# Linear attention and a multiplicative FFN: seven-product gates for two more chunks, sums kept in PSUM, one-instruction minima, and a new order

## The chip, the cores and the metric

The kernel runs on one core of one Trainium2 chip. The core has five engines that follow their own instruction queues: TensorE (PE, with its weight loads shown apart as PEld), VectorE (DVE), ScalarE (ACT), GpSimd (POOL) and SyncE (SP), of which POOL here only starts transfers and SP starts transfers alone. The metric is the time of one execution on the device in microseconds; the lower the better. A change is judged by the median of several runs against the kernel before.

## The reference

Eight sequences of 576 tokens go through a linear attention of 8 heads of 64, and the 4608 rows that come out go through a feed-forward block whose two halves are multiplied:

```python
def phi(x):
    return np.where(x > 0, x, np.exp(x) - 1.0) + 1.0
q_p, k_p = (phi(q), phi(k))
kv = np.einsum('bhsd,bhse->bhde', k_p, v)
z = np.sum(k_p, axis=2)
num = np.einsum('bhsd,bhde->bhse', q_p, kv)
den = np.einsum('bhsd,bhd->bhs', q_p, z)[..., None] + 1e-06
attn = num / den            # (8, 8, 576, 64), then rows of 512
a = x @ w1                  # (4608, 512) @ (512, 1024)
b = x @ w2
h = a * b @ w3              # 1024 x 1024
out = h @ w_out             # 1024 -> 512
```

## The kernel before

The rows are handled in nine chunks of 512. Chunk b below 8 holds the first 512 rows of sequence b; the last 64 rows of all eight sequences form chunk 8. Inputs and outputs are float32, the products are bf16 with float32 sums in PSUM. `w3 @ w_out` is made once, at the start, and kept as `wf_sb`, so a chunk needs two gate products with w1 and w2 and one output product.

The program is not scheduled by a tool: a long string, ORDER, lists its steps, and each engine gets its instructions in the order in which the steps stand there. A step is a letter, the chunk, and a part. A "+" behind a step moves its elementwise work to another engine (its transfers to POOL's queue). The letters that matter here:

- L, M, N and R load k, q, v and the 64-row tails of a sequence; each big load is 512 KB into one of 13 buffers of the pool `ld`. T and D are transposing copies from SBUF to SBUF, started by SP, S and H store rows of the output. SP works through its transfers in the order of the string.
- x, y, z (for k) and X, Y, Z (for q) make phi as min(exp(x), max(x, 0) + 1): ACT's exponential (line 179), DVE's maximum (line 184), DVE's minimum (line 209, two instructions of 128x512 for each half of the heads). v casts the values to bf16 (line 215, ACT).
- K sums k and v over the sequence on PE into `kvp` and ACT copies it to SBUF. A is a normalisation of 128 rows: PE writes numerator and denominator into the PSUM tile `nd`, DVE adds 1e-6 (line 324), takes the reciprocal (325) and multiplies (326).
- F is one gate unit of 128 of the 1024 hidden columns for 512 rows: 4 + 4 matmuls of 128x512 (line 362), an ACT copy of a to SBUF (367), a DVE product with b (368). Chunks 0 to 5 are done with eight F each (for two of chunk 0's and chunk 1's sixteen units the same work is split into steps h and i).
- G is the other way to make gates, used for chunks 6, 7 and 8: the matrices are cut into 2 x 2 blocks and seven block products, with sums and differences of blocks, take the place of eight. For each of four column blocks q there are products 1 to 7, each with four matmuls of 128x256 (line 422), for a and b side by side in one PSUM bank. Products 1, 3, 5 and 7 pile up in one bank (`gu`); after 1 and 3 ACT copies the state to SBUF (line 450). Products 4 and 6 pile up in another bank, product 2 had a bank of its own (`gt`). Sums of an SBUF copy and a bank are DVE's (line 454), and m steps multiply a by b from SBUF (465). Product 7's a half is copied by ACT (458) and multiplied by DVE with its b half in PSUM (459). The block differences come from steps e (weights, line 396) and d (rows, 407).
- O is an output unit of 128 rows: eight matmuls of 128x512 (line 536) and a copy.

PSUM has eight banks: four for F and for G's `gt` banks, two for G's `gu` and O's sums, and a pair for `nd` and `kvp`. The SBUF sums of G live in a ring of 12 half buffers cut from six `ld` buffers.

Of the kernel before, what the change touches and what calls it, by code (L numbers as in the profile page):

```python
# [8 lines left out]
F32 = mybir.dt.float32  # L9
# [11 lines left out]
def kernel(  # L21
# [41 lines left out]
    ones = consts.tile([P, 2], BF16)  # L63
    w1_sb = wpool.tile([P, KC, DFF], BF16)
# [134 lines left out]
    def phi_min(name, b, g):  # L199
# [7 lines left out]
        e, y = (t.rearrange("p (c u j d) -> p c u j d", c=2, u=2, d=D) for t in (e, y))  # L207
        for c in range(2):
            nc.vector.tensor_tensor(out=p[0][:, 2 * g + c].rearrange("p j u d -> p u j d"),  # L209
                                    in0=e[:, c], in1=y[:, c], op=ALU.min)  # L210
# [60 lines left out]
    def q_tr(b, g, alt):  # L271
# [9 lines left out]
        for i in range(2):  # L281
# [4 lines left out]
            out=qts[b, 0][:, 2 * g:2 * g + 2, :].rearrange("p i (j t) -> p (i j) t", t=P), in_=tp)  # L286

    def nat(b, j):
# [35 lines left out]
        nc.vector.tensor_scalar_add(out=r[rows], in0=v4[:, :, :, D], scalar1=1e-6)  # L324
# [110 lines left out]
    def g_unit(c, q, i):  # L435
# [3 lines left out]
        a, m, name, first = ((), ((0, 0, 0), (0, 0, 0), "u", True), ((0, 0, 1), (0, 1, 0), "t", True),  # L439
# [8 lines left out]
        if i in (1, 3, 4):  # L448
            s = st["s", i] = fsm("gs")
            nc.scalar.copy(out=s, in_=t)  # L450
        elif i in (2, 5, 6):
            s = st["c", i] = fsm("gc")
            o = st["s", {2: 1, 5: 4, 6: 3}[i]]
            nc.vector.tensor_tensor(out=s, in0=o, in1=t, op=ALU.add)  # L454
            ring.append(o)
        else:
            s = fsm("ga")
            nc.scalar.copy(out=s[:, 0], in_=t[:, 0])
            nc.vector.tensor_mul(out=abs_[c][:, q + 4, 0:HN], in0=s[:, 0], in1=t[:, 1])
            ring.append(s)  # L460

    def g_mul(c, q, i, alt):
        s = cs_[c, q]["c", i]
        f, r = {2: (q, 0), 5: (q + 4, 1), 6: (q, 1)}[i]
# [121 lines left out]
    A1.4 x2.1 F1.7 F1.6 x2.2 y2.2 z2.2 N2.1 y3.2 x3.2 O0.3 F1.0 Y2.0 X2.0 Z2.0 N2.0 y2.1 F1.1 v2.1+  # L586
    R2.1+ z2.1 L2.0 y2.0 v2.2 F1.5 R3.1+ x2.0 z2.0 M3.0 v2.0 F1.4 O0.2 X3.0 K2 Y3.1 v3.2+ Z3.1 O0.1
    Y3.0 Z3.0 T2.0 A2.3 F1.2 A2.2 N3.0 F1.3 v3.0 L3.1 z3.2 L3.0 x3.0 x3.1 y3.0 S0.1 y3.1 O0.0 N3.1
    T3.0 A2.1 R6.0+ v3.1 O1.1 z3.0 A2.0 O1.0 D2.0 R4.0+ S1.0 z3.1 K3 O1.2 A3.0 O1.3 A3.3 F2.5 F2.3
    A3.2 F2.0 M5.1 Y5.1 R5.1+ R4.1+ y4.2 S1.1 F2.2 M4.1 A3.1 R5.0+ D3.0 x4.2 z4.2 M4.0 F2.1 Y4.1  # L590
    N4.1 F2.4 R6.1+ L4.1 e0.0 A2.4 v4.2 L4.0 F2.6 e0.2 F2.7 X5.1 Z5.1 A3.4 F3.3 X4.0 Y4.0 Z4.0 O2.3+
    X4.1 y5.2 v4.1 y4.1 F3.1 y6.2 Z4.1 x4.1 F3.4 z4.1 v5.2 y4.0 x4.0 F3.0 N4.0 z4.0 F3.5 v4.0 O2.2+
    M5.0 X5.0 K4 v6.2+ e0.1 T4.0 F3.7 x5.2 z5.2 L5.1 x5.1 Y5.0 Z5.0 y5.1 F3.2 S0.0 A4.1 F3.6 L5.0
    y5.0 O2.1 N5.0 x5.0 A4.0 v5.0 O2.0 z5.1 N5.1 S2.1 A4.2 T5.0 v5.1 O3.3 z5.0 A4.3 D4.0 O3.2+ K5
    S3.1 O3.1 A5.3 M6.1 O3.0 A5.0 F4.0 X6.1 A5.2 F4.7 M6.0 X6.0 Y6.0 Z6.0 D3.1 F4.2 F4.4 A5.1 F4.5
    e1.0 F4.3 L6.1 y6.1 x6.1 A4.4 R7.0 L6.0 y6.0 y7.2 D5.0 F4.1 x6.0 F4.6 z6.0 Y6.1 Z6.1 F5.6 x6.2
    z6.2 z6.1 F5.5 N6.1 v6.1 N6.0 A5.4 e1.1 e1.3 M7.0 X7.0 F5.7 S2.0 F5.4 Y7.0 O4.2+ v6.0 K6 O4.3
# [132 lines left out]
```

## Time and profile before

| what | value |
|---|---|
| time, median of 3 runs | 246.97 us (246.8 to 249.23) |
| the profiled execution | 247.36 us |
| its span, first to last instruction | 245.6 us |
| mean granted TensorE clock | 0.993 |
| HBM read and written | 38.80 MB and 9.44 MB |

The profile is one execution. A stretch of time is given from the start of the span. A row of the instruction groups has the line, engine, operation, tiles and shape, the count, then busy time in us, the mean of one in ns, and behind the bar the engine's idle time ahead of these instructions with what ended it. A row of the waits has who waited, for whom, the sum in us, how often, and the longest. Neighbours on one engine overlap a little at their ends, so a group's busy time may be below its count times its mean.

### The profile page before, as it was taken

The page shows a single profiled execution, that of the slowest core. Times are in us where ns is not written, and L with a number is a line of the kernel's source. Part 1 is how long each engine was busy: PE and PEld are TensorE (multiplying, and loading weights), DVE is VectorE, ACT ScalarE, POOL GpSimd, SP SyncE. Part 2 cuts the span into 40 slices and gives each one's busy share as a digit, 9 for nine tenths or more (in the row PEclk, how much of TensorE's full clock was granted, in tenths as well). Part 3 has the DMA queues.
Part 4 walks back from the last instruction along what each step waited for, and adds up shares of the span by engine and source line. Part 5 has one row for each costly group of instructions (what it writes and reads, how often), then busy time and mean ns, then how long its engine had stood idle before and what let it go on. Part 6 is the DMA issues. An engine that isn't in the chain of part 4 may idle for free.

```text
span 245.6 us, 4278 instructions
## 1 busy us (share of the span) xinstructions
PE 229.7 (94%) x1548; PEld 133.2 (54%) x1548; DVE 184.7 (75%) x425; ACT 136.4 (56%) x222; POOL 44.8 (18%) x73
## 2 busy tenths in 40 slices
PE   0689968999999999999999999999999999999994
PEld 0345555654454554444545444454498686788542
DVE  3227979677698837989794589958999996989721
ACT  2207777658775715498663456736776285455220
POOL 8445467660000096200000000000000000000000
PEclk9999997999999999999999999999999999999999
DMA  6999999999869799798997989989980151040074
GB/s 152 192 201 299 297 250 243 198 274 280 274 126 350 152 247 313 166 348 225 275 308 153 256 221 242 280 231 328 209 247 0 23 144 29 0 175 0 3 171 171
DMA packets 65461, 49.43 MB, mean 201 GB/s; under 512 B 34016, under 2 KB 60384, under 8 KB 65440
## 3 DMA queue, kind: packets, MB, share of 16 engines
q1 hardware_dynamic: 54560, 36.71, 55.4%
q0 software_dynamic: 10736, 12.33, 25.1%
q8 instruction: 12, 0.20, 0.3%
q10 hardware_dynamic: 144, 0.13, 0.2%
q14 instruction: 9, 0.07, 0.1%
HBM read 38.80 MB, written 9.44 MB: 196 GB/s over the span
## 4 chain that ended last, share of the span: by engine, by line
PE 83%; DMA 13%; ACT 2%; issue 1%; POOL 0%; ACTq 0%; POOLq 0%
PE o_ps L536 25%; PE a_ps L362 17%; PE b_ps L362 17%; PE gu L422 9%; PE gt L422 6%; DMA q<-in_q_dram 5%; DMA k<-in_k_dram 5%; PE nd L310 4%; DMA wt_sb<-in_moe_w_out_dram 3%; PE kvp L245 2%; ACT e L179 1%; PE o_ps L561 1%; PE kvp L249 1%; PE xtp L341 1%; POOL w3b L137 0%
## 5 line engine op out<-in xcount | busy, mean ns | idle before, releaser
L536 PE MATMUL o_ps<-wf_sb,ab 128*128 128x512 bf16 x280 | 64.7, 379 | 0.0
L362 PEld LDWEIGHTS <-w_sb 128*128 128x128 bf16 x384 | 36.6, 98 | 40.2 <-issue 0.6
L362 PE MATMUL a_ps<-xt,w_sb 128*128 128x512 bf16 x192 | 50.8, 382 | 0.0
L362 PE MATMUL b_ps<-xt,w_sb 128*128 128x512 bf16 x192 | 50.2, 379 | 0.0
L536 PEld LDWEIGHTS <-ab 128*128 128x128 bf16 x280 | 26.9, 98 | 29.1 <-DVE ab L465 0.3
L368 DVE TENSOR_TENSOR ab<-a_sb,b_ps 128x512 bf16<-128x512 f32 x48 | 32.4, 684 | 13.0 <-PE b_ps L362 6.5
L367 ACT COPY a_sb<-a_ps 128x512 f32<-128x512 f32 x48 | 27.5, 585 | 21.5 <-PE a_ps L362 20.2
L538 ACT COPY o_sb<-o_ps 128x512 f32<-128x512 f32 x27 | 15.6, 586 | 34.6 <-PE o_ps L536 24.9
L326 DVE TENSOR_TENSOR xn<-nd,r 128x512 bf16<-128x512 f32 x30 | 20.7, 691 | 1.0
L422 PEld LDWEIGHTS <-spare 128*128 128x128 bf16 x192 | 18.6, 97 | 2.4
L179 ACT ACTIVATE e<-q 128x1024 bf16<-128x1024 f32 x16 | 16.8, 1058 | 5.0 <-DMA q<-in_q_dram 4.9
L310 PE MATMUL nd<-kv,qt 128*128 128x130 bf16 (+1 forms) x160 | 15.9, 221 | 2.8 <-DVE xn L326 1.7
L454 DVE TENSOR_TENSOR spare<-spare,gt 128x512 f32<-128x512 f32 x24 | 16.0, 682 | 2.8 <-ACT spare L450 2.3
L310 PEld LDWEIGHTS <-qt 128*128 128x128 bf16 (+1 forms) x160 | 11.5, 99 | 11.6 <-DVE xn L326 3.0
L154 PE MATMUL wf_ps<-wt_sb,w3t 128*128 128x512 bf16 x64 | 16.1, 394 | 1.1 <-DMA wt_sb<-in_moe_w_out_dram 0.8
L179 ACT ACTIVATE e<-k 128x1024 bf16<-128x1024 f32 x16 | 16.9, 1060 | 0.2 <-DMA k<-in_k_dram 0.2
L450 ACT COPY spare<-gu 128x512 f32<-128x512 f32 x24 | 13.4, 590 | 3.4 <-PE gu L422 2.8
L422 PEld LDWEIGHTS <-w_sb 128*128 128x128 bf16 x144 | 14.0, 98 | 2.4
L465 DVE TENSOR_TENSOR ab<-spare 128x256 bf16<-128x256 f32 x36 | 13.7, 419 | 0.1
L114 POOL DMA_DIRECT2D qk32r<-in_q_dram x12 | 7.6, 636 | 33.5 <-ACT o_sb L538 30.9
L324 DVE TENSOR_SCALAR r<-nd 128x8 f32<-128x8 f32 (+1 forms) x38 | 6.1, 162 | 10.0 <-PE nd L310 9.9
L209 DVE TENSOR_TENSOR qj<-e,y 128x512 bf16<-128x512 bf16 x32 | 12.1, 421 | 1.7 <-ACT e L179 0.9
(87 smaller groups left out, 301.9 us busy)
## 6 DMA issues: line engine op xcount, KB each, us to landing
out_dram<-o_sb SPq DMA_DIRECT2D x15, 512.0 KB, 4.3
q<-in_q_dram SPq DMA_DIRECT2D x13, 512.0 KB, 6.8
k<-in_k_dram SPq DMA_DIRECT2D x12, 512.0 KB, 6.9
v<-in_v_dram SPq DMA_DIRECT2D x12, 512.0 KB, 7.7
w3b<-in_moe_w_dram POOLq DMA_DIRECT2D x8, 256.0 KB, 10.1
k<-in_k_dram POOLq DMA_DIRECT2D x4, 512.0 KB, 8.5
w_sb<-in_moe_w_dram POOLq DMA_DIRECT2D x8, 256.0 KB, 7.8
q<-in_q_dram POOLq DMA_DIRECT2D x3, 512.0 KB, 11.0
```

The lines of the kernel that those rows point to most:

```text
L154: nc.tensor.matmul(wfs[i], w3ts[i][:, kc, :], wo_sb[:, kc, :], start=(kc == 0), stop=(kc == FC - 1))
L179: nc.scalar.activation(out=e, in_=x, func=AF.Exp)
L310: nc.tensor.matmul(nds[g][rows, i * 2 * E1:(i + 1) * 2 * E1], w, kvs[b % 2][:, i, g].rearrange("p u e -> p (u e)"), start=True, stop=True)
L326: nc.vector.tensor_tensor(out=dst.rearrange("p (g h) e -> p g h e", g=2), in0=v4[:, :, :, 0:D], in1=r[rows].unsqueeze(3).to_broadcast([n, ...
L362: nc.tensor.matmul(ps, w[:, kc, f * P:(f + 1) * P], xt_of(c)[:, :, kc, :], start=(kc == 0), stop=(kc == KC - 1))
L367: nc.scalar.copy(out=a_sb, in_=a_ps)
L368: nc.vector.tensor_mul(out=abs_[c][:, f, :], in0=a_sb, in1=b_ps)
L422: nc.tensor.matmul(t[:, w], l, r, start=(first and w == 0 and k == 0), stop=(k == 1), skip_group_check=True)
L454: nc.vector.tensor_tensor(out=s, in0=o, in1=t, op=ALU.add)
L465: (nc.gpsimd if alt else nc.vector).tensor_mul(out=abs_[c][:, f, r * HN:(r + 1) * HN], in0=s[:, 0], in1=s[:, 1])
L536: nc.tensor.matmul(o_ps, ab[:, f, m * P:(m + 1) * P], wf_sb[:, f, :], start=(f == 0), stop=(f == FC - 1))
L538: copy_of(alt)(out=rows_of(c, m // 2)[:, m % 2], in_=o_ps)
```

## The change

Five things change.

Chunks 4 and 5 are made by G steps, too, so F is left to chunks 0 to 3. Their block differences (steps d4 and d5) take two more `ld` buffers; to make room the differences of w1 move into `wt_sb`, which held w_out at the start, and the ring shrinks from 12 to 8 half buffers.

Sums are made in place: after product 1, ACT copies the bank `gu` to a second PSUM bank, `gt`, and product 2's matmuls add to that copy, so that the sum of products 1 and 2 needs no DVE instruction. It is then multiplied as product 7 is: ACT copies the a half to SBUF, DVE multiplies with the b half in PSUM. Sums 5 and 6 overwrite the SBUF copy that they add to.

```diff
-        a, m, name, first = ((), ((0, 0, 0), (0, 0, 0), "u", True), ((0, 0, 1), (0, 1, 0), "t", True),
+        a, m, name, first = ((), ((0, 0, 0), (0, 0, 0), "u", True), ((0, 0, 1), (0, 1, 0), "t", False),
...
-        if i in (1, 3, 4):
+        if i == 1:
+            st["t"] = mm_ps.tile([P, 2, HN], F32, tag="mm", name="gt")
+            nc.scalar.copy(out=st["t"], in_=t)
+        elif i in (3, 4):
             s = st["s", i] = fsm("gs")
             nc.scalar.copy(out=s, in_=t)
-        elif i in (2, 5, 6):
-            s = st["c", i] = fsm("gc")
-            o = st["s", {2: 1, 5: 4, 6: 3}[i]]
-            nc.vector.tensor_tensor(out=s, in0=o, in1=t, op=ALU.add)
-            ring.append(o)
+        elif i in (5, 6):
+            s = st["c", i] = st["s", {5: 4, 6: 3}[i]]
+            nc.vector.tensor_tensor(out=s, in0=s, in1=t, op=ALU.add)
         else:
-            s = fsm("ga")
-            nc.scalar.copy(out=s[:, 0], in_=t[:, 0])
-            nc.vector.tensor_mul(out=abs_[c][:, q + 4, 0:HN], in0=s[:, 0], in1=t[:, 1])
-            ring.append(s)
+            s = sm.tile([P, NCH], F32, tag="f", name="a_sb", bufs=4)[:, 0:HN]
+            nc.scalar.copy(out=s, in_=t[:, 0])
+            nc.vector.tensor_mul(out=abs_[c][:, q if i == 2 else q + 4, 0:HN], in0=s, in1=t[:, 1])
```

Phi's minimum of half the heads is one instruction of 128x1024 in place of two of 128x512. For that, phi is stored with the row group j outermost, so that the output runs through memory and the inputs are read in runs of 64. What reads it later (the transposes, the blocks of `qt`) follows.

```diff
-        e, y = (t.rearrange("p (c u j d) -> p c u j d", c=2, u=2, d=D) for t in (e, y))
-        for c in range(2):
-            nc.vector.tensor_tensor(out=p[0][:, 2 * g + c].rearrange("p j u d -> p u j d"),
-                                    in0=e[:, c], in1=y[:, c], op=ALU.min)
+        e, y = (t.rearrange("p (h j d) -> p j h d", j=NJ, d=D) for t in (e, y))
+        nc.vector.tensor_tensor(out=p[0][:, 2 * g:2 * g + 2].rearrange("p c j u d -> p j (c u) d"),
+                                in0=e, in1=y, op=ALU.min)
```

For 21 of the 40 normalisations the small sum with 1e-6 is ACT's, with the constant in a column `eps`; those are the A steps that the new order writes with a "+".

```diff
-        nc.vector.tensor_scalar_add(out=r[rows], in0=v4[:, :, :, D], scalar1=1e-6)
+        if alt:
+            nc.scalar.add(out=r[rows], in_=v4[:, :, :, D], add=eps[rows])
+        else:
+            nc.vector.tensor_scalar_add(out=r[rows], in0=v4[:, :, :, D], scalar1=1e-6)
```

And ORDER is new from the last gate steps of chunk 1 on. One line of it before and one after, from the middle:

```diff
-    S3.1 O3.1 A5.3 M6.1 O3.0 A5.0 F4.0 X6.1 A5.2 F4.7 M6.0 X6.0 Y6.0 Z6.0 D3.1 F4.2 F4.4 A5.1 F4.5
+    Z6.0 z6.0 O3.2 A5.0 x6.1 e1.3 O3.1 M7.0 L7.1 y6.1 A5.2 S3.1 O3.0 G4.1.1 d4.0 D1.1 G4.1.4 d4.1
```

Three places show what that does to the engines' queues. First ACT, behind the sums of k and v of sequence 5, where chunk 4's gates begin. Before:

```order
L254 CAST kv_109<-kvp 64x4x65 x2
L538 COPY o_sb<-o_ps 128x512 x2
L367 COPY a_sb<-a_ps 128x512
L179 ACTIVATE e<-q_1752 128x1024
L367 COPY a_sb<-a_ps 128x512
L179 ACTIVATE e<-q_1811 128x1024
L367 COPY a_sb<-a_ps 128x512 x4
```

After, in the middle of chunk 4's gates, with the cast of chunk 6's v (v_1858 and v_1878 are its two loads):

```order
L458 COPY gt<-gu 128x512 x2
L461 COPY spare<-gu 128x512 x2
L461 COPY spare<-gt_1951 128x512
L216 CAST vt_105<-v_1858 128x4x4x64
L467 COPY a_sb<-gt 128x256
L467 COPY a_sb<-gu 128x256 x2
L467 COPY a_sb<-gt 128x256
L216 CAST vt_105<-v_1878 128x4x4x64
```

Where one copy for each F step stood between exponentials, five copies for each column block of G now stand around the casts, and a cast that waits holds them up.

Second SP's queue ahead of those two loads of v. Before (v_1980 and v_1983):

```order
L114 DMA qk32r<-in_k_dram 64x4x64 x2
L104 DMA k_1905<-in_k_dram 128x4x256
L351 DMA_TRANSPOSE xt<-xn 128x16x128
L104 DMA v_1980<-in_v_dram 128x4x256
L104 DMA v_1983<-in_v_dram 128x4x256
L104 DMA q_1997<-in_q_dram 128x4x256
```

After:

```order
L106 DMA q_1765<-in_q_dram 128x4x256
L106 DMA k_1767<-in_k_dram 128x4x256
L554 DMA out_dram<-o_sb 128x1024
L355 DMA_TRANSPOSE xtr<-xnr 128x4x128
L116 DMA v32r<-in_v_dram 64x4x64 x2
L106 DMA v_1858<-in_v_dram 128x4x256
L106 DMA v_1878<-in_v_dram 128x4x256
L355 DMA_TRANSPOSE xtr<-xnr 128x4x128
L355 DMA_TRANSPOSE xt<-xn 128x16x128
```

Two loads of chunk 7 (q_1765 and k_1767) and a store have moved ahead of the loads of v, and the transposing copy of chunk 5's rows has moved behind them.

Third DVE, at the normalisations of sequence 3 between gate units of chunk 2. Before:

```order
L324 TENSOR_SCALAR r<-nd 128x8
L325 RECIPROCAL r<-r 128x8
L326 TENSOR_TENSOR xn<-nd,r 128x512
L368 TENSOR_TENSOR ab<-a_sb,b_ps 128x512 x2
L324 TENSOR_SCALAR r<-nd 128x8
L325 RECIPROCAL r<-r 128x8
L326 TENSOR_TENSOR xn<-nd,r 128x512
```

After:

```order
L372 TENSOR_TENSOR ab<-a_sb,b_ps 128x512
L329 RECIPROCAL r<-r 128x8
L330 TENSOR_TENSOR xn<-nd,r 128x512
L372 TENSOR_TENSOR ab<-a_sb,b_ps 128x512
L329 RECIPROCAL r<-r 128x8
L330 TENSOR_TENSOR xn<-nd,r 128x512
```

The small sum with 1e-6 is gone from DVE's queue; it stands in ACT's, and the reciprocal now waits for ACT.

78 lines of the change are left out of this document (44 added, 34 removed).

## The prediction, made before the changed kernel ran

> **What bounds the kernel now.** I read the page's engine shares and its chain of waits first, then the table of stretches, then the chain in order of time.
>
> ```profile
> PE 229.7 (94%) x1548; PEld 133.2 (54%) x1548; DVE 184.7 (75%) x425; ACT 136.4 (56%) x222; POOL 44.8 (18%) x73
> PE 83%; DMA 13%; ACT 2%; issue 1%; POOL 0%; ACTq 0%; POOLq 0%
> 46.80:160.40 113.60, 113.60 (x663) 56.47 (x662) 90.18 (x205) 70.06 (x109) 16.05 (x26) 1.00 0.96 249
> 160.40:178.40 18.00, 18.00 (x113) 9.20 (x111) 14.18 (x36) 10.83 (x17) 0.00 (x0) 1.00 0.91 250
> 180.00:200.00 20.00, 20.00 (x177) 16.19 (x176) 19.25 (x47) 12.10 (x24) 0.00 (x0) 1.00 0.25 83
> 131.50:178.40 46.90, 46.90 (x276) 23.36 (x274) 36.64 (x83) 26.58 (x41) 0.00 (x0) 1.00 0.95 248
> 242.00:245.60 3.60, 0.00 (x0) 0.00 (x0) 0.00 (x0) 0.37 (x1) 0.00 (x0) 1.00 0.37 135
> ```
>
> The columns of a stretch are its length, then the busy time of PE, PEld, DVE, ACT and POOL, the granted clock, the DMA share and GB/s. From 46.8 us (the end of step K1) PE is busy in every stretch, at full clock. A busy PE could still hide gaps, since its records overlap, so I add its steps up at the chain's prices, in the rows below. Behind K1 stand 46 gate units (steps F, and two as h) of 0.86 + 0.86, 1.73 us before rounding; 35 output units (O) of 12.09 / 7 = 1.73; 84 products (G) of 0.87 / 2 = 0.437; 35 normalisations (A) of 0.23; 6 sums of k and v (K) of 179.53 - 178.40 = 1.13; 4 transposes of about 0.2 and the last piece of 1.76. That is 79.6 + 60.6 + 36.7 + 8.1 + 6.8 + 0.9 + 1.8 = 194.5 us of the 195.2 from 46.8 to 242.0. There is next to no slack to win: only less PE work shortens this part, and any new wait of PE lengthens it. The DMA queues are the second full resource: a share of 0.96 until 160.4. DVE follows, at 19.25 of 20 us in one stretch, in which PE lost nothing.
>
> ```profile
> 108.78 0.86 PE a_ps L362 x4
> 109.64 0.86 PE b_ps L362 x4
> 160.37 0.45 PE kvp L245 x8
> 178.40 0.45 PE kvp L245 x8
> 179.53 0.87 PE gu L422 x8
> 181.28 0.87 PE gu L422 x8
> 182.59 0.23 PE nd L310 x4
> 228.16 12.09 PE o_ps L536 x56
> 240.25 1.76 PE o_ps L561 x16
> ```
>
> **The change part by part.** *Seven products for chunks 4 and 5.* Each loses 8 F steps of 1.73 us on PE, 13.8 us, and gets 28 G steps of 0.437 us, 12.2 us. Two chunks: 27.7 - 24.5 = 3.2 us less PE work, all of it on the path. No other PE step is added or removed, and the weight loads of the G steps (16.19 us of 20 in the stretch from 180) already lie inside the 0.437.
>
> The other engines pay:
>
> ```profile
> L368 DVE TENSOR_TENSOR ab<-a_sb,b_ps 128x512 bf16<-128x512 f32 x48 | 32.4, 684 | 13.0 <-PE b_ps L362 6.5 <-ACT a_sb L367 5.2 <-PE tpr L277 0.7
> L367 ACT COPY a_sb<-a_ps 128x512 f32<-128x512 f32 x48 | 27.5, 585 | 21.5 <-PE a_ps L362 20.2 <-DVE ab L368 1.1
> L454 DVE TENSOR_TENSOR spare<-spare,gt 128x512 f32<-128x512 f32 x24 | 16.0, 682 | 2.8 <-ACT spare L450 2.3 <-PE gt L422 0.4
> L465 DVE TENSOR_TENSOR ab<-spare 128x256 bf16<-128x256 f32 x36 | 13.7, 419 | 0.1
> L450 ACT COPY spare<-gu 128x512 f32<-128x512 f32 x24 | 13.4, 590 | 3.4 <-PE gu L422 2.8 <-DVE ab L459 0.5
> L459 DVE TENSOR_TENSOR ab<-spare,gu 128x256 bf16<-128x256 f32 x12 | 5.0, 416 | 0.1
> L458 ACT COPY spare<-gu 128x256 f32<-128x256 f32 x12 | 4.5, 372 | 6.7 <-PE gu L422 5.2 <-DVE spare L454 1.2 <-DVE ab L465 0.2
> L407 DVE TENSOR_TENSOR spare<-xt,spare 128x512 bf16<-128x512 bf16 x4 | 1.7, 422 | 0.1
> ```
>
> A chunk by F costs DVE 8 x 0.684 = 5.5 us and ACT 8 x 0.585 = 4.7. By G in the new form, each of four column blocks costs DVE two sums (0.683), two products with PSUM (0.416) and two of SBUF (0.419), 3.04 us, so 12.1 and 4 differences of 0.42, 13.8 us; ACT three copies of 0.590 and two of 0.372, 2.51 us, so 10.1. Chunks 4 and 5 together: DVE +16.7, ACT +10.7 us.
>
> *Sums in place.* For the 12 blocks of chunks 6 to 8, product 2 now adds to a PSUM copy of product 1. DVE loses a sum and an SBUF product and gains a PSUM product, 0.683 + 0.419 - 0.416 = 0.69 us, 8.2 us in all; ACT gains one 0.372 copy each, 4.5 us. No row shows ACT writing PSUM: nearest is the same copy to SBUF, 0.590; a gain or a loss of 0.2 us each way over 20 blocks stays on ACT, beside PE, as long as other G steps stand between a block's products 1 and 2. They do: at least three other steps of PE stand between them.
>
> *Phi's minimum.*
>
> ```profile
> L209 DVE TENSOR_TENSOR kj<-e,y 128x512 bf16<-128x512 bf16 x32 | 12.0, 417 | 0.5 <-ACT e L179 0.5
> L396 DVE TENSOR_TENSOR spare<-w_sb 128x1024 bf16<-128x1024 bf16 x4 | 2.7, 683 | 0.0
> L324 DVE TENSOR_SCALAR r<-nd 128x8 f32<-128x8 f32 x30 | 4.9, 162 | 9.9 <-PE nd L310 9.9
> L179 ACT ACTIVATE er<-qk32r 128x512 bf16<-128x512 f32 x8 | 5.0, 634 | 7.4 <-DMA qk32r<-in_k_dram 7.4
> L179 ACT ACTIVATE e<-k 128x1024 bf16<-128x1024 f32 x16 | 16.9, 1060 | 0.2 <-DMA k<-in_k_dram 0.2
> ```
>
> Two instructions of 0.417 (12.0 / 32 = 0.375 each when back to back) become one, by the row of the same size 0.683: 32 x (0.75 - 0.68) = 2.2 us off DVE. With inner runs of 64 elements on the inputs in place of the output I expect no other rate; 0.419 at 512 and 0.683 at 1024 elements are 0.52 ns an element, and at half that rate DVE would pay 32 x 0.53 = 17 us, enough to make it the bound.
>
> *Eps by ACT.* 21 of the normalisations lose DVE's 0.162 us (3.4 us) and gain an ACT instruction of 8 elements. Two ACT sizes bound it: 634 at 512 and 1060 at 1024 elements give 0.83 ns an element and 0.21 us at nothing; the copies, 372 at 256 and 590 at 512, give 0.16. I take 0.21, 4.5 us; 0.16 to 0.37 are the ends. The Trainium skill, "ScalarE: Activation LUTs", section "What ACT_TABLE_LOAD costs", says that a bias held in a one-column operand, as here, costs some 93 ns more; by its formula it is an estimated 0.29 us, 6.0 us in all.
>
> Sums: DVE +16.7 - 8.2 - 2.2 - 3.4 = +2.9 us, ACT +10.7 + 4.5 + 4.5 = +19.7 us, from 184.7 and 136.4 busy. Both stay below PE's 226.5. So what decides is where it falls. Between K5 and K7 the old order gives DVE 40.7 us of instruction means, and the trace has 36.64 busy (0.90, since neighbours overlap). The new order puts 65 G steps in this stretch: 50.4 us by the same means, 45.4 at 0.90, against 46.9 of PE. That is 97%, like the 96% from 180 to 200 us that cost PE nothing.
>
> *The new order.* The stretch up to the last steps of chunk 1's gates is as before, so the first 46.8 us stay, and so does the 3.6 us tail. For new stalls I allow 0.4 us: there was none in 195 us before, but both DVE and ACT are now fuller. The sum: span 245.6 - 3.2 + 0.4 = 242.8. The profiled execution took 247.36 us, 1.76 around the span, so 244.6; it lies 0.39 above the median of the runs, 246.97, so **244.2** as a median.
>
> **The rivals.** *The loads come late, and it is slower.*
>
> ```profile
> 148.37 1.16 SPq L104 DMA_DIRECT2D v<-in_v_dram  x2
> 154.40 1.05 ACT L215 CAST vt<-v 128x1024 bf16<-128x1024 f32 x1
> 156.41 1.06 ACT L179 ACTIVATE e<-q 128x1024 bf16<-128x1024 f32 x1 [0.96 <-DMA q<-in_q_dram]
> 158.31 1.06 ACT L215 CAST vt<-v 128x1024 bf16<-128x1024 f32 x1
> DMA to landing us min/median/max: 4.5/7.7/12.9
> ```
>
> Between K1 and K6 the new order has 28 F, 36 G and 16 O steps and 24 normalisations for 40 F, 17 O and 25 before: 36 x 0.437 - 12 x 1.73 - 1.73 - 0.23 = -7.0 us of PE work. K6 stood at 160.37 and is due at 153.4, the cast of chunk 6's v at 147.4 instead of 154.4. But v was issued at 148.37 and cast 6 us later. Ahead of it stand nearly the same transfers, by the order three plain ones more (2.1 us each at 249 GB/s) and one transposing copy less (some 4 us). The share of 0.96 leaves 4.5 us of DMA idle until 160.4. So v lands 7.0 - 4.5 = 2.5 us late if every gap can be filled, 7.0 if none, plus about 2 for the extra transfers, less 2.2 us for five products that stand behind the cast and do not need ACT: 2.3 to 6.8 us of PE wait at one cast that holds ACT's queue, 4.5 in the middle. Time: 247.36 - 3.2 + 4.5 - 0.4 = 248.3 (246.1 to 250.6). It turns slower than before from 3.2 us on. For it: the DMA share, and the exponential at 156.41, which already waited 0.96 us for a load. Against it: the new order also asks for loads earlier between K1 and K5, where the gaps are.
>
> *DVE becomes the bound between K5 and K7.* If the instructions there do not overlap, 50.4 - 46.9 = 3.5 us are lost: 247.36 - 3.2 + 3.5 - 0.4 = 247.3; half of it, 245.5. Against it stands the stretch from 180.
>
> *The eps hop is exposed.* Nearly all normalisations share one PSUM tile, and PE already waits for it at times:
>
> ```profile
> DVE r L324 <- PE nd L310: 9.9, 7, 3.0
> PE nd L310 <- DVE xn L326: 1.7, 2, 1.0
> ```
>
> With ACT in the chain, each gets longer by the dearer instruction (0.05 us) and by what stands ahead on ACT, up to an exponential of 1.06; I take 0.35. At 9 of 21 exposed the gain is gone; at a quarter, 1.8 us, the time is 245.6; at all, 7.4 us, 251.2. The Trainium skill, "ScalarE: Activation LUTs", section "Rules for kernel authors", advises additions on VectorE rather than ScalarE; by that rule this part of the change is the wrong way round. The trace agrees on the bare price, 0.162 on DVE, but DVE is the fuller engine.
>
> **How the numbers follow.** About 1% is what a measurement of this kernel tells from no change: 244.5 and 249.4 are the edges. The forecast (243.6 to 245.2) has a chance of 0.48, of which 0.38 lies below 244.5; loads late 0.22, half of it beyond 249.4; DVE-bound 0.15, nearly all within the edges; the eps hop 0.15, a third of it beyond 249.4, a fifth below 244.5. That gives 0.42 faster, 0.40 the same, 0.18 slower. The range from 243.4 to 249.8 leaves out about 0.05 below and 0.15 above.
>
> **What would show it.** Right: PE's busy time from K1 to its last matmul falls to 192 us and no PE wait over 0.5 us appears; the forecast's own steps show as G rows near 109 ns a matmul, minima near 0.68 us, ACT's 128x8 rows at 0.2 to 0.3. The loads: ACT idle before a cast or an exponential, released by DMA, with PE waiting behind it. DVE: no idle from K5 to K7 and PE released by DVE sums. The eps hop: PE waiting on "nd". It is wrong altogether if PE's own steps change price, the products that add to a bank written by ACT above all.

## The result, and the profile after

| | before | after |
|---|---|---|
| median of 4 runs | 247.28 us (246.8 to 249.23) | 254.34 us (253.69 to 255.64) |
| ratio, 95% interval | | 1.0277 (1.0204 to 1.035) |
| the profiled execution, its span | 247.36 us, 245.6 us | 254.89 us, 253.1 us |
| mean granted TensorE clock | 0.993 | 0.976 |

The changed kernel is slower by 2.8%. The forecast was 244.2 us in a range up to 249.8. Four kernels below had one run more than 1.5% above their fastest (258.75 us in e2, 256.69 in e3, 256.33 in e10, 739.6 in e14), which the ratios leave out and without which their medians are 254.61, 253.75, 253.23 and 250.3 us.

From the page of the changed kernel, first the engines' busy shares, then the chain of waits, then the row of the granted clock and the DMA share over the 40 slices (6.33 us each):

```profile
PE 229.6 (91%) x1627; PEld 142.1 (56%) x1644; DVE 187.8 (74%) x401; ACT 153.5 (61%) x279; POOL 45.4 (18%) x73
PE 73%; DMA 21%; ACT 2%; issue 1%; POOL 0%; ACTq 0%; POOLq 0%
PEclk9999997999999999959999999999999999999998
DMA  7999999999999999999997997954607320440145
```

PE's busy time is what it was (229.7), though it has 3.2 us less to do, and in the chain PE's share has fallen from 83 to 73% while DMA's has risen from 13 to 21%. The clock has a 5 in one slice, which it did not have before. The waits of PE longest in total, behind those of the weights at the start, are these (who waited, for whom, the sum, how often, the longest):

```profile
PE a_ps L366 <- DMA xt<-xn: 3.1, 1, 3.1
PE nd L311 <- DMA qt<-qj: 2.2, 2, 1.8
PE nd L311 <- DVE xn L330: 1.9, 2, 1.2
```

Both DMA waits are for transposing copies from SBUF to SBUF: `xt`, the rows of chunk 3 (step D3.0), and `qt`, phi of q of sequence 6 (T6.0). The timeline of PE around the first (start, length, what, and in brackets the idle time ahead):

```profile
104.36 1.03 PE L366 MATMUL b_ps<-xt,w_sb 128*128 128x512 bf16 x4
...
108.80 1.89 PE L366 MATMUL a_ps<-xt,w_sb 128*128 128x512 bf16 x4 [3.07 <-DMA xt<-xn]
110.48 1.91 PE L366 MATMUL b_ps<-xt,w_sb 128*128 128x512 bf16 x4
```

SP's rows for the two copies, from its own timeline:

```profile
100.13 4.59 SPq L355 DMA_TRANSPOSE xt<-xn  x1
157.15 4.07 SPq L270 DMA_TRANSPOSE qt<-qj  x1
```

PE stands still for 3.07 us and then needs 1.9 us for four matmuls that took 1.03. The copy into `xt` landed 8.6 us after its issue, the longest of the six such copies. The times to landing of all six, first in the changed kernel, then before:

```profile
DMA to landing us min/median/max: 4.3/4.6/8.6
DMA to landing us min/median/max: 4.3/4.4/5.0
```

Its place hardly differs. Before the change SP issued the same copy at

```profile
99.16 2.92 SPq L351 DMA_TRANSPOSE xt<-xn  x1
```

and PE came to chunk 3's first gate unit 6.0 us later, at 105.15; in the changed kernel PE was ready for it at 105.73, 5.6 us after the issue. A copy of at most 5.0 us would have been in time in both. It was not the only slow transfer: the loads of 512 KB that were issued from 80 to 104 us took 7.5 to 11.5 us to land (medians of q, k and v), against 5.0 to 6.4 before.

The table of stretches (length; busy time of PE, PEld, DVE, ACT, POOL; clock; DMA share; GB/s) has for the kernel before:

```profile
87.00:120.00 33.00, 33.00 (x183) 16.02 (x182) 25.93 (x57) 19.49 (x33) 10.49 (x17) 1.00 0.95 256
120.00:160.00 40.00, 40.00 (x228) 19.61 (x226) 32.19 (x73) 22.92 (x35) 0.00 (x0) 1.00 0.98 251
```

and for the changed kernel:

```profile
87.00:120.00 33.00, 29.82 (x166) 14.40 (x167) 23.66 (x44) 18.47 (x33) 10.20 (x16) 0.90 1.09 258
120.00:160.00 40.00, 39.84 (x291) 26.15 (x293) 37.04 (x81) 30.09 (x58) 0.00 (x0) 1.00 0.99 242
```

The DMA share was 0.95 and 0.98 before; now it is 1.09 and 0.99, and PE lost 3.2 us of the first stretch. (A share above 1 stands as the profile gives it; why it passes 1 is not shown.) To say where the time went I cut the execution at the first matmuls of each K step. Expected is the length of before plus the difference in PE steps between the two orders, at the prices of the prediction (from K3 to K4, for instance, two F and two O units fewer, 4 x 1.73 = 6.92 us less).

| stretch, us | before | PE work | after | lost |
|---|---|---|---|---|
| start to K2 | 72.42 | 0 | 72.92 | 0.5 |
| K2 to K3 | 12.54 | +1.73 | 14.27 | 0.0 |
| K3 to K4 | 32.29 | -6.92 | 31.39 | 6.0 |
| K4 to K6 | 42.96 | -1.80 | 41.51 | 0.4 |
| K6 to K7 | 18.03 | +5.75 | 25.82 | 2.0 |
| K7 to the last matmul's end | 63.77 | -1.97 | 62.49 | 0.7 |
| from there to the end | 3.59 | 0 | 4.70 | 1.1 |

10.7 us are lost, 3.2 saved, and 245.6 + 7.5 = 253.1. The largest loss is the pause for `xt` with the slow matmuls behind it; the second holds the pause for `qt`.

### The profile page after: what moved, and what is told of

Same layout as the page of the kernel before. It is cut to its first block, busy times and chain, and to the rows that moved or that the text cites. A ratio compares the mean times of both kernels' runs of the same rounds, so it can differ in the third digit from the quotient of the medians.

```text
span 253.1 us, 4494 instructions
## 1 busy us (share of the span) xinstructions
PE 229.6 (91%) x1627; PEld 142.1 (56%) x1644; DVE 187.8 (74%) x401; ACT 153.5 (61%) x279; POOL 45.4 (18%) x73
## 4 chain that ended last, share of the span: by engine, by line
PE 73%; DMA 21%; ACT 2%; issue 1%; POOL 0%; ACTq 0%; POOLq 0%
PE o_ps L544 23%; PE gu L429 12%; PE a_ps L366 11%; PE b_ps L366 11%; PE gt L429 9%; DMA qt<-qj 5%; DMA k<-in_k_dram 5%; DMA q<-in_q_dram 4%; DMA xt<-xn 3%; PE nd L311 3%; DMA wt_sb<-in_moe_w_out_dram 3%; PE kvp L246 2%; ACT e L181 1%; PE o_ps L569 1%; ACT xt L346 1%
## 5 line engine op out<-in xcount | busy, mean ns | idle before, releaser
L366 PE MATMUL a_ps<-xt,w_sb 128*128 128x512 bf16 x128 | 36.5, 403 | 3.1 <-DMA xt<-xn 3.1
L366 PE MATMUL b_ps<-xt,w_sb 128*128 128x512 bf16 x128 | 35.8, 397 | 0.0
L372 DVE TENSOR_TENSOR ab<-a_sb,b_ps 128x512 bf16<-128x512 f32 x32 | 21.7, 684 | 12.6 <-PE b_ps L366 10.0
L371 ACT COPY a_sb<-a_ps 128x512 f32<-128x512 f32 x32 | 18.4, 584 | 14.1 <-PE a_ps L366 14.0
L429 PEld LDWEIGHTS <-wt_sb 128*128 128x128 bf16 x160 | 15.3, 98 | 2.6
L429 PEld LDWEIGHTS <-spare 128*128 128x128 bf16 x160 | 15.6, 98 | 1.8
L464 DVE TENSOR_TENSOR spare<-spare,gu 128x512 f32<-128x512 f32 x20 | 13.5, 684 | 4.0 <-PE gu L429 2.9
L429 PE MATMUL gu<-spare 128*128 128x256 bf16 x80 | 15.3, 272 | 0.0
L429 PE MATMUL gu<-spare,wt_sb 128*128 128x256 bf16 x80 | 15.3, 272 | 0.0
L464 DVE TENSOR_TENSOR spare<-spare,gt 128x512 f32<-128x512 f32 x20 | 13.4, 683 | 1.5 <-PE gt L429 1.0
```

What stands on the lines that cost most here:

```text
L366: nc.tensor.matmul(ps, w[:, kc, f * P:(f + 1) * P], xt_of(c)[:, :, kc, :], start=(kc == 0), stop=(kc == KC - 1))
L371: nc.scalar.copy(out=a_sb, in_=a_ps)
L372: nc.vector.tensor_mul(out=abs_[c][:, f, :], in0=a_sb, in1=b_ps)
L429: nc.tensor.matmul(t[:, w], l, r, start=(first and w == 0 and k == 0), stop=(k == 1), skip_group_check=True)
L464: nc.vector.tensor_tensor(out=s, in0=s, in1=t, op=ALU.add)
```

## The experiments

Steps are named as in ORDER. The theories: *A*, two transfers stand at bad places, and mending them mends the kernel. *D*, the order asks for transfers earlier than the full DMA engines can bring them, so behind each late one stands the next. *Q*, it is SP's queue, where each transfer waits for all that stands ahead of it. And for the other parts of the change: the hop of eps to ACT, and phi's minimum. The ratios are against the kernel before in the same round, whose median went from 247.28 to 248.48 us between rounds; "lost" is reckoned as in the table above, from each kernel's profile.

**e1_fill: work ahead of the first pause.** Two output units that need no transfer, and a store, move ahead of the unit that waits.

```diff
-    X4.1 Z4.1 v4.2 x4.1 N4.1 y4.1 F3.2 F3.7 z4.1 M6.1 X6.1 S1.1 v5.2+ v4.1 X5.0 Y5.0 Z5.0 M5.1 Y5.1
-    O2.2 x6.2 T4.0 F3.3 R5.0+ e0.2 K4 y5.2 F3.0 A4.3+ x5.2 z5.2 O2.3 Y6.1 Z6.1 e0.3 F3.5 A4.2+ L5.1
+    X4.1 Z4.1 v4.2 x4.1 N4.1 y4.1 S1.1 O2.2 O2.3 F3.2 F3.7 z4.1 M6.1 X6.1 v5.2+ v4.1 X5.0 Y5.0 Z5.0 M5.1 Y5.1
+    x6.2 T4.0 F3.3 R5.0+ e0.2 K4 y5.2 F3.0 A4.3+ x5.2 z5.2 Y6.1 Z6.1 e0.3 F3.5 A4.2+ L5.1
```

> The changed kernel with the store S1.1 and the output units O2.2 and O2.3 of chunk 2 moved ahead of chunk 3's first gate unit, behind which the transposing copy of chunk 3's rows is awaited. Theory A (the loss is the late copy there, 3.1 us of PE wait and 3.1 us more at the lowered clock): the two units, 3.5 us, fill the wait, PE does not pause, the clock stays at 1.00, and the time falls by 5 to 6 us, to 248.3 to 249.3. Rival B (ACT's and DVE's longer queues are the cause, and the copy is only the last link): the wait moves elsewhere and the time falls by less than 1.5 us. Rival C (the wait matters but not the clock): it falls by about 3 us, to 251.3.

Measured: 254.16 us (253.25 to 255.26), 1.026 of before (1.0216 to 1.0305). The wait for `xt` is gone, and K3 to K4 takes 28.16 us instead of 31.39, though it holds one O unit more (1.73): 5.0 us won. But K4 to K5 loses 2.2 us (0.1 without the move), and K6 to K7 takes 28.10 in place of 25.82, with a longer wait for `qt`,

```profile
PE nd L311 <- DMA qt<-qj: 2.4, 1, 2.4
PE o_ps L544 <- DVE ab L372: 1.8, 2, 0.9
```

and K7 begins at 186.59, later than the 185.91 without the move. 1.3 us of that lie ahead of K2, where the two orders are the same; behind K2, 4.3 of the 5.0 us won were lost again. The place was right, and the time came back elsewhere: against A.

**e2_t6: the second copy earlier.** T6.0 moves to right behind A4.4, in SP's queue ahead of four loads of tails (R7.0) and a store (S3.0).

```diff
-    d5.2 G4.2.6 v6.0 m4.2.6 A4.4+ G5.0.1 G5.1.1 d5.3 G5.1.4 G5.0.3 G5.0.2 G5.1.3 G5.0.4 G5.0.5 X7.0
-    m4.3.5 K6 G5.1.5 G5.1.2 R7.0 S3.0 G5.0.7 T6.0 A6.3+ G5.0.6 M7.1 x7.1 G5.1.7 X7.1 v7.2 m5.0.6
+    d5.2 G4.2.6 v6.0 m4.2.6 A4.4+ T6.0 G5.0.1 G5.1.1 d5.3 G5.1.4 G5.0.3 G5.0.2 G5.1.3 G5.0.4 G5.0.5 X7.0
+    m4.3.5 K6 G5.1.5 G5.1.2 R7.0 S3.0 G5.0.7 A6.3+ G5.0.6 M7.1 x7.1 G5.1.7 X7.1 v7.2 m5.0.6
```

> The changed kernel with the transposing copy of chunk 6's q (T6.0) issued right behind the last normalisation of chunk 4, ahead of the q and k tails of sequence 7 and of a store on SP's queue. Theory A: it starts some 3.5 us earlier (at about 153.5 in place of 157.2), the 1.8 us that PE waits for it go, and the time falls by 1.5 to 2 us, to about 252.5. Rival B (PE there is held by DVE, which is full from K5 to K7): the copy lands earlier, but the time stays within 0.7 us of 254.3.

Measured: 254.76 us (251.92 to 258.75), 1.0244 (1.0178 to 1.0311); the profiled execution is the quickest of these, 251.92. In it the wait for `qt` is 0.3 us, but ACT now waits for chunk 7's q, and PE behind it for a copy by ACT (first from ACT's waits, then from PE's):

```profile
ACT e L181 <- DMA q<-in_q_dram: 6.2, 6, 2.6
```

```profile
PE gu L429 <- ACT o_sb L546: 1.8, 1, 1.8
```

One late transfer has taken the place of another; no gain in the median.

**e3_eps_dve: all eps back on DVE.**

```diff
-        if alt:
-            nc.scalar.add(out=r[rows], in_=v4[:, :, :, D], add=eps[rows])
-        else:
+        if True:
             nc.vector.tensor_scalar_add(out=r[rows], in0=v4[:, :, :, D], scalar1=1e-6)
```

> The changed kernel with all sums with 1e-6 on DVE again, the order unchanged. Rival B (the hop over ACT lengthens the normalisations and delays what hangs on them, the transposing copies among them): the time falls by 1.5 us or more, to below 252.8. Theory A (the hop is hidden, and costs what it takes off DVE): the time stays within 1 us of 254.3, 0.16 us x 21 = 3.4 us more on DVE and 0.27 x 21 = 5.6 us less on ACT beside PE.

Measured: 254.29 us (252.38 to 256.69), 1.0238 (1.0184 to 1.0291), with the same two waits, 2.8 and 2.1 us. The difference from the changed kernel lies within the spread: in the new order the hop costs nothing that can be measured.

**e4_old_order and e7_old_order_phi: the small parts alone.** The order, the gates and the sums of before, with phi's minimum in one instruction, w1's differences in `wt_sb`, and in e4 also eps on ACT for the same 21 normalisations (one of the lines):

```diff
-    S3.1 O3.1 A5.3 M6.1 O3.0 A5.0 F4.0 X6.1 A5.2 F4.7 M6.0 X6.0 Y6.0 Z6.0 D3.1 F4.2 F4.4 A5.1 F4.5
+    S3.1 O3.1 A5.3+ M6.1 O3.0 A5.0 F4.0 X6.1 A5.2 F4.7 M6.0 X6.0 Y6.0 Z6.0 D3.1 F4.2 F4.4 A5.1 F4.5
```

> The kernel before, in its own order, with three of the five parts: phi's minimum in one instruction, the sum with 1e-6 by ACT for the same 21 normalisations, and w1's differences in the buffer of w_out; chunks 4 and 5 by F and the sums by DVE as before. Theory A (these parts cost nothing, the order does): 246.5 to 247.8, as the kernel before. Rival B (the parts themselves slow the path): 249 or more.

> The kernel e4_old_order with the sums with 1e-6 on DVE again: the old order with phi's minimum in one instruction and w1's differences in the buffer of w_out. If the hop over ACT alone cost e4_old_order its 14 us (its trace has DVE waiting 22.1 us for ACT's sums): 246.5 to 248. If phi's new layout or the buffer has a part in it: 250 or more.

Measured: e4 261.94 us (261.54 to 262.57), 1.0581 (1.0547 to 1.0615); e7 249.15 (247.6 to 250.15), 1.0027 (0.9994 to 1.006). Phi and the differences cost nothing that can be told from the spread. In the old order the hop alone costs 261.94 - 249.15 = 12.8 us. From the waits of e4:

```profile
DVE r L329 <- ACT r L326: 22.1, 11, 8.1
PE nd L311 <- DVE xn L330: 10.4, 6, 4.3
ACT o_sb L546 <- DMA out_dram<-o_sb: 9.7, 2, 5.4
```

Read from the bottom: an output copy on ACT waits for a store to free its buffer, the eps sum stands behind it in ACT's queue, DVE's reciprocal waits for that, and PE for DVE. e7 has the same waits of output copies for stores (9.7 us, the longest 5.6), and without the hop nothing hangs on them. So the new order is what makes the hop free.

**e5_cut_after and e6_cut_before: fewer bytes.** Of the ten stores of chunks 0 to 4 only 16 of 128 partitions are written, in the changed kernel and in the one before; the rest of these output rows is left out. That is 10 x 512 KB x 7/8 = 4.6 MB less to move, with the order and all waits as they were.

```diff
-            nc.sync.dma_start(out=dst[:, 2 * r + m0:2 * r + m1, :], in_=o_sb[:, m0:m1])
+            n = 16 if c < 5 else P
+            nc.sync.dma_start(out=dst[0:n, 2 * r + m0:2 * r + m1, :], in_=o_sb[0:n, m0:m1])
```

> The changed kernel with the ten stores of chunks 0 to 4 cut to 16 of the 128 partitions (the rest of those output rows is left out): each is still issued at its place and still waits, but 4.6 MB less move, some 18 us of transfer time at 253 GB/s, all before about 180 us. Theory D (up to 155 us the transfers are at their limit, so whatever a new place gains is lost at the next late one): K7 moves from 186 to 180 or earlier and the time falls by 4 us or more, to below 250.5. Theory A (two places where the order gives a copy too little lead): less than 2 us. Theory Q (it is the order on SP's queue that is late, not the transfers): less than 1 us.

> The kernel before with the same ten stores cut to 16 partitions. All theories: PE is full from K1 on, so the time stays within 1 us of 247.5; if it falls by 2 us or more, transfers also held the kernel before, and the comparison with the changed kernel says less.

Measured: e5 249.49 us (247.47 to 250.9), 1.0057 (1.0005 to 1.0108), 4.8 us less than the changed kernel; e6 248.15 (246.69 to 249.14), 1.0003 (0.9978 to 1.0028), no gain. From e5, a row of its table of stretches, SP's row of the copy into `xt`, and PE's wait for it:

```profile
120.00:160.00 40.00, 39.84 (x313) 27.81 (x315) 37.52 (x83) 31.17 (x59) 0.00 (x0) 1.00 0.88 215
```

```profile
99.86 4.69 SPq L355 DMA_TRANSPOSE xt<-xn  x1
```

```profile
PE a_ps L366 <- DMA xt<-xn: 1.1, 1, 1.1
```

The copy is issued at the same place, 99.86 for 100.13, and takes as long to issue, but lands 6.6 us later instead of 8.6. So here the load of the DMA engines made it late, by 2.0 us at least, and before the change this load held nothing up. That is for D, and against A and a Q that does without the bytes. The issue alone still took 4.69 us, against 2.92 before the change; why is not shown.

**e8_fill_t6: both moves.** The diffs of e1 and e2 together.

> The changed kernel with both moves, that of e1_fill and that of e2_t6. Theory A (the places add up): 3.1 + 3.1 us at the copy of chunk 3's rows and 1.8 at chunk 6's q go, so about 248 to 249. Theory D (the transfers set when K7 comes): 252 or more, with the waits at other transfers.

Measured: 257.51 us (256.27 to 257.97), 1.0399 (1.036 to 1.0438): worse than either. K6 to K7 takes 29.45 us. ACT waits for chunk 7's q, here in its timeline, and PE stands for 4.0 us behind it, for a copy by ACT:

```profile
167.09 1.06 ACT L181 ACTIVATE e<-q 128x1024 bf16<-128x1024 f32 x1 [4.78 <-DMA q<-in_q_dram]
```

**e9_cut_fill_t6: both moves with fewer bytes.** e8 with the cut stores of e5.

> The two moves together (S1.1, O2.2 and O2.3 ahead of F3.2; T6.0 right behind A4.4), now with the ten stores of chunks 0 to 4 cut to 16 of 128 partitions, so 4.6 MB less to transfer and most of these output rows left unwritten. Theory D (the transfers are at their limit, and each late one that is removed shows the next): with room in the queues the moves have nothing behind them that becomes late, so they help now; the two waits of PE for xt and qt are gone, and of the 249.5 us of the cut alone 1 to 3 us go: 246.5 to 248.5. Rival P (the two moves are bad places by themselves, whatever the transfers do, as their sum of 257.5 us with full stores could also be read): the loss of 3.2 us against the new order stays, 252 or more.

Measured: 253.15 us (252.4 to 253.65), 1.0201 (1.0165 to 1.0237). That is the rival's number: with room in the DMA engines (their share from 120 to 160 us is 0.73) the moves still cost 253.15 - 249.49 = 3.7 us. D alone falls. e9 loses 2.1 us more than e5 from K6 to K7, and 1.8 us more from K4 to K5. ACT waits 3.75 us for the same load of q. SP's rows in e9:

```profile
146.77 2.71 SPq L355 DMA_TRANSPOSE xt<-xn  x1
153.16 2.71 SPq L270 DMA_TRANSPOSE qt<-qj  x1
...
160.55 0.41 SPq L106 DMA_DIRECT2D q<-in_q_dram  x1
```

SP starts nothing from 149.5 to 153.16, where T6.0 is next and not yet free to go; then four tail loads and a store come ahead of q. It is issued 3.9 us behind K6 (156.63), in the changed kernel 1.2 us behind it.

**e10_busy_pause: the pause filled with useless work.** In the changed kernel, ahead of the unit that waits for `xt`:

```diff
         a_ps, b_ps = f_open(c, f)
+        for n in range(14 if (c, f) == (3, 2) else 0):
+            nc.tensor.matmul(a_ps, w1_sb[:, n % KC, 0:P], w2_sb[:, n % KC, 0:NCH], start=True, stop=True)
```

> The changed kernel with 14 matmuls of 128x512 added ahead of unit F3.2, on weights that are there, into the bank that the unit then overwrites: some 3.0 us of useless PE work in place of the 3.07 us pause at the transposing copy of chunk 3's rows. Theory C (the pause itself halves the granted clock for the matmuls after it): PE still starts the unit at the same time, but its quartets of matmuls take 1.03 us instead of 1.89, K3 to K4 takes about 28.3 us instead of 31.4, and the whole 251 to 252 if nothing else becomes late, up to 254.5 if the next transfers then are late by as much. Rival T (the clock is lowered by something else at that place): quartets of 1.9 us again, K3 to K4 31 us or more, 254 to 257 in all.

Measured: 254.23 us (251.89 to 256.33), 1.022 (1.0131 to 1.0308). PE's timeline:

```profile
105.81 3.19 PE L377 MATMUL a_ps<-w_sb 128*128 128x512 bf16 x13
108.84 1.03 PE L366 MATMUL a_ps<-xt,w_sb 128*128 128x512 bf16 x4
109.70 1.03 PE L366 MATMUL b_ps<-xt,w_sb 128*128 128x512 bf16 x4
```

The unit starts at the same 108.8 us, but its matmuls run at full clock, and K3 to K4 takes 28.41 us in place of 31.39. So the pause cost twice: 3.07 us of waiting and 3.0 of half clock. The median fell by less than the spread of its runs. In the profiled execution, one of the two quicker runs, K7 begins 2.0 us earlier and the span is 251.5, so 1.6 us of the 3.0 were left at the end there.

**e11_cut_fill and e12_fill_t6_q7: which of the moves, and why.** e11 is e5 with the first move alone. e12 is e8 (all bytes) with one load taken ahead: chunk 7's q (M7.1) now stands right behind T6.0 in SP's queue, the tail loads and the store behind it.

```diff
-    m4.3.5 K6 G5.1.5 G5.1.2 R7.0 S3.0 G5.0.7 A6.3+ G5.0.6 M7.1 x7.1 G5.1.7 X7.1 v7.2 m5.0.6
+    m4.3.5 K6 G5.1.5 G5.1.2 G5.0.7 A6.3+ G5.0.6 M7.1 R7.0 S3.0 x7.1 G5.1.7 X7.1 v7.2 m5.0.6
```

> The first move alone (S1.1, O2.2 and O2.3 ahead of F3.2) with the ten stores of chunks 0 to 4 cut to 16 of 128 partitions. The cut alone took 249.5 us, the cut with both moves 253.2, where the exponential on chunk 7's q waited 3.75 us: T6.0, put right behind A4.4, waits there for A4.4 to be done with the tile qt, and SP issued q 2.7 us later after K6 than in the changed kernel. Theory D+Q (transfers at their limit, and SP's strict order beside it): the first move is harmless where the queues have room, 248 to 250, K6 to K7 about 25 us. Rival P (the first move is a bad place by itself): 251.5 or more, with PE waiting for gate products or o_sb between K4 and K5 or K6 and K7.

> Both moves with full stores, and the load of chunk 7's q also ahead of R7.0 (four tail loads) and S3.0 (a store), right behind T6.0 in SP's queue. Theory Q (in that kernel, 257.5 us, q came late because of what stood ahead of it in SP's queue): q is issued some 3.5 us earlier, ACT's wait of 4.8 us for it goes to 1.5 or less, PE's wait of 4.0 us for o_sb goes, K6 to K7 falls from 29.5 to 26.5 us or less, and the whole to 253 to 254.5. If nothing else came late in turn, even 251. Theory D alone (the transfers themselves were too slow, whatever SP's order): q lands as late, or the four tail loads or the store take its place as the wait, and it stays at 256 or more.

Measured: e11 249.53 us (248.62 to 251.83), 1.006 (1.0016 to 1.0105), so the first move as a whole costs nothing where there is room: against e5 it wins 1.0 us from K3 to K4 and 1.0 from K6 to K7, and loses 1.8 from K4 to K5. e12 250.58 us (250.52 to 251.59), 1.0112 (1.0053 to 1.017): 6.9 us less than e8, better than expected. SP's rows of e8:

```profile
153.89 2.68 SPq L270 DMA_TRANSPOSE qt<-qj  x1
156.88 1.27 SPq L116 DMA_DIRECT2D qk32r<-in_q_dram  x2
...
160.47 0.55 SPq L554 DMA_DIRECT2D out_dram<-o_sb  x1
161.06 0.42 SPq L106 DMA_DIRECT2D q<-in_q_dram  x1
```

and of e12, with its row of the table of stretches:

```profile
153.40 2.69 SPq L270 DMA_TRANSPOSE qt<-qj  x1
156.18 0.54 SPq L106 DMA_DIRECT2D q<-in_q_dram  x1
```

```profile
120.00:160.00 40.00, 38.04 (x298) 25.96 (x298) 37.42 (x82) 29.82 (x56) 0.00 (x0) 1.00 1.04 250
```

The load is issued 4.9 us earlier. The exponential's longest wait for a load of q falls from 4.8 to 2.1 us, PE's wait of 4.0 us is gone, and K6 to K7 takes 23.84 us, which is its length before plus its PE work (18.03 + 5.75 = 23.78). The DMA engines are as full as ever (1.04). So it is Q here: the bytes were not too many for this place, they were issued in the wrong order. The Trainium skill, "DMA: Bandwidth & Descriptors", section "Anatomy of one DMA — SWDGE (gpsimd) path", says that a semaphore wait happens on the issuing sequencer, before dispatch; e9 agrees, with the loads that stood behind a copy that could not go yet.

**e13_tail and e14_tail_half_fill: what is left.** Both build on e12. In e13 the output units of chunk 8 and their eight small stores go ahead of O7.0, O7.1 and S7.0:

```diff
-    G7.3.5 G7.2.2 G7.2.7 G7.2.6 G7.3.6 G7.3.7 O7.0 O7.1 O8.0 S7.0 m7.2.5 m7.1.5 O8.1+ m8.3.5 O8.2
-    S8.0 m7.0.5 m7.2.6 m7.1.6 m7.3.6 O8.3 H8.3 H8.2 m7.3.5 O7.2+ H7.2 Q7.3
+    G7.3.5 G7.2.2 G7.2.7 G7.2.6 G7.3.6 G7.3.7 O8.0 m8.3.5 O8.1+ m7.2.5 O8.2 m7.1.5
+    S8.0 m7.0.5 O8.3 H8.2 m7.2.6 H8.3 O7.0 m7.1.6 O7.1 m7.3.6 S7.0 m7.3.5 O7.2+ H7.2 Q7.3
```

In e14, on top of that, O2.3 goes back to its place between K4 and K5.

> The kernel with both moves and q ahead (250.6 us), and at the end the output units of chunk 8 and their eight small stores ahead of O7.0, O7.1 and the store S7.0, as in the kernel before. Theory Q (in the new order SP is still starting the eight stores, 7.6 to 7.8 us of its queue, when the last pieces of chunk 7 are copied, so these are issued late): the time from the last matmul's end to the end falls from 4.85 to 3.6 us, the whole from 250.6 to 249.4 (249.0 to 249.8). Rival (the tail is set by the landing of whatever is last, or PE loses as much because the units of chunk 8 cover the last gate products less well): no gain, 250.3 or more.

> As e13, but O2.3 stays at its place between K4 and K5, and only S1.1 and O2.2 are ahead of F3.2. If the loss between K3 and K5 (0.6 and 2.3 us in the kernel with q ahead) is a shortage of work that does not wait for transfers, it is shared out: PE waits for the copy of chunk 3's rows about 1.3 us, too short to lower the clock, and K4 to K5 gains 1 to 2 us, so 0 to 1 us less in all than e13. If it is the transfers' amount alone, the two stretches together take as long as in e13, and the total stays within 0.5 us of it.

Measured: e13 250.06 us (249.67 to 250.89), 1.0097 (1.006 to 1.0134); e14 250.5 us, 1.0087 (1.0049 to 1.0124). SP's last rows in the changed kernel:

```profile
240.38 7.58 SPq L559 DMA_DIRECT2D out_dram<-o_sb  x8
248.06 0.53 SPq L554 DMA_DIRECT2D out_dram<-o_sb  x1
248.69 0.39 SPq L574 DMA_DIRECT2D out_dram<-o_sb  x1
```

and in e13:

```profile
234.10 6.29 SPq L559 DMA_DIRECT2D out_dram<-o_sb  x8
242.74 2.23 SPq L554 DMA_DIRECT2D out_dram<-o_sb  x2
245.18 0.33 SPq L574 DMA_DIRECT2D out_dram<-o_sb  x1
```

In the changed kernel the eight small stores held SP until 247.96, and the last store behind them began only after PE's last matmul had ended at 248.40. In e13 the time from the last matmul's end (245.57) to the end (249.1) is 3.5 us, as before the change. The tail is settled; of the 1.3 us only 0.5 shows in the medians, which is within their spread.

e14 comes out as e13 in the medians, but its profile shows what the loss from K4 to K5 is. With O2.3 back at its place it is 0.6 us. In the six kernels that have O2.3 ahead of K4 (e1, e8, e9, e11, e12, e13) it is 1.9 to 2.4, and in the changed kernel, e2, e3, e5 and e10, which leave the unit alone, 0.1 to 0.4. There the unit had filled waits of PE for a normalisation and a gate product. From e13, and in e14 no longer there:

```profile
122.43 0.40 PE L311 MATMUL nd<-kv,qt 128*128 128x130 bf16 x4 [0.57 <-DVE xn L330]
133.75 1.04 PE L544 MATMUL o_ps<-wf_sb,ab 128*128 128x512 bf16 x4 [0.88 <-DVE ab L372]
```

So the first move paid for the late copy with work that was needed some 15 us later. In return K3 to K4 loses 1.9 us in e14 and 1.0 in e13; the 0.8 us that remain are too few to show in the medians.

No kernel with the new order was faster than the kernel before. The best that write all of the output, e13 and e14, are 1% slower. In e12's profile 6.3 us are still lost by the table's reckoning: 1.3 in the tail, 2.35 between K4 and K5, 0.85 from K5 to K6, 0.65 from K3 to K4, 0.7 behind K7 and 0.4 at the head. The 2.35 are for the most part the missing O2.3; e11, with fewer bytes, has 1.9 there, so bytes are not their main cause. In e14's profile 5.0 us are left, of which 1.9 lie between K3 and K4; what they come from stays open.

## Why the prediction was wrong

*What bounds the kernel before*: held. PE is full from K1 on, and the table's expected lengths, made from the prediction's prices, come out to 0.2 us in the three stretches without a late transfer (K2 to K3, K4 to K5, K5 to K6).

*Gates of chunks 4 and 5, -3.2 us of PE*: held. The price of G's matmuls did not change, product 2's, which add to a bank written by ACT, included: the last row below has 272 ns each, and 273 was the mean of the same row before; 3.2 us less work is what the table balances with.

*The other engines' prices*: held. From the instruction groups after (busy time, mean ns, idle time behind the bar):

```profile
L210 DVE TENSOR_TENSOR kj<-e,y 128x1024 bf16<-128x1024 bf16 x16 | 11.0, 688 | 1.1 <-ACT e L181 0.5
L458 ACT COPY gt<-gu 128x512 f32<-128x512 f32 x20 | 11.5, 579 | 2.3 <-PE gu L429 2.1
L326 ACT ACTIVATE r<-nd,eps 128x8 f32<-128x8 f32 x16 | 4.3, 268 | 6.2 <-PE nd L311 6.1
L429 PE MATMUL gt<-xt,w_sb 128*128 128x256 bf16 x64 | 9.4, 272 | 0.0
```

Minima were forecast at 0.683 and took 0.688; the copy to PSUM 0.590 and 0.579; eps 0.21, with 0.37 as the upper end, and 0.268. The 0.29 that the prediction worked out from the Trainium skill ("ScalarE: Activation LUTs", section "What ACT_TABLE_LOAD costs") was the nearer. DVE is busy for 187.8 us (187.6 forecast).

*"For new stalls I allow 0.4 us"*: this is the step that failed. It reads 10.7 us in the table: 6.0 from K3 to K4 (3.07 of waiting for the copy of chunk 3's rows and 3.0 at half clock), 2.0 from K6 to K7 (1.79 of them waiting for `qt`), 1.1 in the tail, behind the eight small stores, and 1.6 elsewhere. The reason given, that 195 us had no stall before, was a property of the old order, in which the transfers landed in time, if only just: chunk 3's rows were needed 6.0 us after the issue of a copy that took at most 5.0; in the new order they were needed after 5.6 and came after 8.6. The prediction counted PE work and engine work of the new order, but not each transfer's time from issue to need, except for one.

*The rival of late loads* had the resource right and the transfer wrong. It worked out one place, v of chunk 6, where no wait came: its rule "4.5 us of DMA idle" said how late the whole is, not which transfer. The first to be late was a transposing copy from 100.13 us on, in a stretch where it had expected the gaps to help; its result, 248.3 us, lacks the second cost (half clock), and SP's strict order, by which a copy that waits holds up the loads behind it (e12: 6.9 us from one load's place).

*DVE as the bound between K5 and K7*: did not come. The stretch K5 to K6, the first half of it, lost 0.2 us, and the losses of the second half went with T6.0's and q's places (e12: 0.1 us left).

*The exposed eps hop*: not in the new order (e3), 12.8 us in the old one (e4 against e7). What makes the size was right, namely what stands ahead on ACT; its bound, an exponential of 1.06 us, was not: an output copy waited 5.4 us for a store.

## What to carry to other kernels

When a change takes work from the bound engine between loads, work out for each transfer in the new order when it is issued, what stands ahead of it in its queue, and when it is needed; a DMA share of 0.96, with which the old order lost nothing, does not tell whether they will be in time, and an added 0.4 us for stalls is not an estimate. Mend late transfers together and in the order of the queue, since one moved ahead holds up those behind it until its own source and buffer are ready. Work that is moved ahead to fill one pause may have been filling another. A pause of PE can cost twice its length, as the 3.07 us here did.

## What the runs showed of the hardware

The clock after a pause: it fell to half after waits of 3.07 us (the changed kernel), 2.41 (e1), 4.01 (e8), and 4.34 and 3.30 (e4), and stayed full after 2.97 (e9) and 2.78 (e3), as after the shorter ones of 1.64 to 2.11 us (the changed kernel, e2, e3, e10). So no single length decides. The Trainium skill, "TensorE: Matmul & The Clock Gate", section "What's actually happening", says that activity is watched in free-running windows of about 3.4 us, and that an idle window halves the clock. Different outcomes for like lengths fit a window that does not start with the pause; the 2.41 us of e1, shorter than that window, do not fit a window that has to be wholly idle. From e9, with no slow row after the pause:

```profile
167.21 0.60 PE L429 MATMUL gu<-xt,w_sb 128*128 128x256 bf16 x4 [2.97 <-ACT o_sb L546]
```

and from e1, with slow ones:

```profile
163.50 0.53 PE L311 MATMUL nd<-kv,qt 128*128 128x130 bf16 x4 [2.41 <-DMA qt<-qj]
164.68 1.06 PE L429 MATMUL gu<-spare,w_sb 128*128 128x256 bf16 x4
```

A transposing copy of one chunk's rows, 4.3 to 5.0 us from issue to landing before, took 8.6 us when it met full DMA engines (a share of 1.09 from 87 to 120 us), and 6.6 us with 4.6 MB of stores taken out. Half of the 8.6 was SP's own time for issuing it, 4.59 us.
